# Layernorm applies ahead of the exponentials of k, k-v products in three groups, and another spread of the W_q folds

## The chip, the cores and the metric

The kernel runs on one core of one Trainium2 chip. The core has five engines with an instruction queue each: TensorE (PE in the profile; its weight loads stand as PEld), VectorE (DVE), ScalarE (ACT), GpSimd (POOL) and SyncE (SP, which here issues every DMA). Each queue runs in order; an instruction that waits for a semaphore holds back what stands behind it on its engine. The metric is device time in microseconds (us) of one execution, lower is better; the time of a kernel is the median of its runs.

## What is computed

Two blocks follow one another on x, 2048 rows of 640 features in bf16: a linear attention with 32 heads of 20 features, and a gated feed-forward of width 1536. Cut to what matters:

```python
qkv = (_layernorm(x) @ wqkv).reshape(B, S, 3, H, Dh)...
q, k, v = qkv[0], qkv[1], qkv[2]
pq = jnp.einsum("bhsd,hdf->bhsf", q, w_phi)
pk = jnp.einsum("bhsd,hdf->bhsf", k, w_phi)
phi_q = jnp.concatenate([_softmax(pq), _softmax(-pq)], axis=-1)
phi_k = jnp.concatenate([_softmax(pk), _softmax(-pk)], axis=-1)
kv = jnp.einsum("bhsf,bhsd->bhfd", phi_k, v)
z  = jnp.einsum("bhsf->bhf", phi_k)
num = jnp.einsum("bhqf,bhfd->bhqd", phi_q, kv)
den = jnp.einsum("bhqf,bhf->bhq", phi_q, z)[..., None] + 1e-6
h = x + (num / den)... @ wo
h2 = h + (_gelu(_layernorm(h) @ w_gate) * (_layernorm(h) @ w_up)) @ w_down
```

The change touches only the first half: the layernorm of x, k and v, the products of phi_k with v, and the preparation of the weights of q.

## The kernel before

The 2048 rows are 16 tiles of 128 rows (`NT`), in four blocks of four tiles. All engines run in the order in which the program names the instructions; nothing reorders them.

**Before the loop** the first tiles are loaded and normalised, their v is made, and W_k is folded with w_phi, so that k's features come out of one projection. That is what `fold` (L213) does for one chunk `d` of 128 rows of a weight: six small matmuls into a PSUM tile `wa` (L227), and a copy from there into the folded weight (L236 on ScalarE). W_q is folded in the loop: `FQ` gives the pass of each of its five chunks, `LQ` the pass in which SP issues the transposing load of the chunk (`load_T`, L186). All copies of W_q's folds are on ScalarE.

**The loop of 16 passes** (L440) is the place of the change. Pass t does, in this order:

1. `k_tile(t)` (L300): ten matmuls of the tile's normalised, transposed rows with the folded W_k into a PSUM tile `pk` (L272), then two exponentials on ScalarE, of pk and of -pk, into `E` (L305). They are called E(t) below.
2. A fold of W_q, if `FQ` has one for t; in pass 15 also the first four pieces of q's projection (`q_mm`, L360) and their exponentials (L365).
3. The k-v products of the tiles that `KVG` names for t (`kv_tile`, L332): 20 matmuls a tile, of E with `vt`, that add up over all 16 tiles in one PSUM tile `kvp` (L338). The tiles that are left follow behind the loop (L486).
4. `v_mm(t + 4)`: ten matmuls of the tile four ahead with W_v into a PSUM tile `pv` (L272). They need `LN1T` of that tile.
5. `ln_ap(t + 6)` (L256): ScalarE normalises the tile six ahead into `ln` (L133), with the bias `mr` that GpSimd has made (L127), and SP issues a DMA that writes its transpose into `LN1T` (L149).
6. `v_ev(t + 4)`: ScalarE copies pv into `vS` (L292).
7. In even passes `ln_st(t + 8, t + 9)` (L252): the statistics of two tiles, on VectorE (L109, L113) and GpSimd (L121, L122, and one `mr` for each tile, L127).
8. `k_norm(t)` (L308): VectorE sums E over the features (`sk`, L312) and takes the reciprocal (`rs`, L316); v is divided by it into `vt` (L320). One half of vt, for tiles of `VP` both, is GpSimd's; VectorE does its half one pass later, behind the sum of the next tile.

From pass 3 (`T3`) on the PSUM holds three tiles of the pool `psG`, which pk, wa, pv and pq take in turn, and `kvp`. A tile of the pool can be written again when the engine that reads it is through. E and vt have eight buffers each, so tile t takes the buffer of tile t - 8.

**Behind the loop** come the rest of the k-v products, `kv_mask` (L342: a small VectorE operation, a copy by ScalarE, and one masked product each on VectorE and GpSimd) into `KV`, the rest of q's projection, and the attention output and feed-forward, in which TensorE is the engine of almost every step.

The plan before the change, by pass:

```python
LQ = (7, 8, 9, 9, 10)
FQ = (10, 11, 12, 13, 14)
KVG = {5: (0, 1), 9: (2, 3, 4, 5), 13: (6, 7, 8, 9), 15: (10, 11)}
```

Of the kernel before, what the change touches and what calls it, by code (L numbers as in the profile page):

```python
# [17 lines left out]
def kernel(  # L18
# [19 lines left out]
    NT = S // P  # L38
# [7 lines left out]
    NH = [(P * c + P - 1) // Dh - H0[c] + 1 for c in range(NC)]  # L46
    VP = (0, 2, 4, 6, 9, 11)
    KA, QA = (0, 2, 4), (0, 1, 2, 3, 4)
    LQ = (7, 8, 9, 9, 10)
    FQ = (10, 11, 12, 13, 14)  # L50

    QG = ((0, 1), (2, 3), (4, 5), (6,), (7, 8), (9, 10), (11, 12), (13, 14), (15,), (16,), (17,), (18,), (19,))
    QT = (15, 15, 15, 15)
    T3 = 3

    KVG = {5: (0, 1), 9: (2, 3, 4, 5), 13: (6, 7, 8, 9), 15: (10, 11)}
    VC = Dh + 1
    KC = Dh + 2

# [39 lines left out]
    def gtile(name):  # L99
        return psG.tile([P, 2, 512], F32, name=name, tag="G")  # L100
# [40 lines left out]
    def transpose_to(dst, src, on_pe, on_dve=False):  # L141

        if on_pe:
            tp = psG.tile([P, 16, P], BF16, name="tp", tag="G")
            for c in range(NC):
                nc.tensor.transpose(tp[:, c, :], src[:, c * P:(c + 1) * P], ident)
            (nc.vector.tensor_copy if on_dve else nc.scalar.copy)(dst, tp[:, 0:NC, :])  # L147
        else:
            nc.sync.dma_start_transpose(dst, src)  # L149
# [63 lines left out]
    def fold(WT, W2, halves, ds=range(NC)):  # L213


        runs = []
        for c in range(NC):
            lo, hi = H0[c] * Dh, (H0[c] + NH[c]) * Dh
            for u in range(2):
                a, b = max(lo, u * HD), min(hi, (u + 1) * HD)  # L220
                if a < b:
                    runs.append((u, c, a, b))
        runs.sort()
        for d in ds:
            wa = gtile("wa")
            for i, (u, c, a, b) in enumerate(runs):
                nc.tensor.matmul(wa[:, u, a - u * HD:b - u * HD], lhsT=WT[:, c, d * P:(d + 1) * P],  # L227
                                 rhs=BD[:, c].rearrange("p a b -> p (a b)")[:, a - H0[c] * Dh:b - H0[c] * Dh],
                                 start=(i == 0 or runs[i - 1][0] != u),
                                 stop=(i + 1 == len(runs) or runs[i + 1][0] != u), skip_group_check=True)  # L230
            dst, src = W2[:, d, :].rearrange("p (u f) -> p u f", u=2), wa[:, :, 0:HD]
            if halves:
                dst = W2[:, d, :].rearrange("p (c u f) -> p u c f", c=NC, u=2)
                src = src.rearrange("p u (c f) -> p u c f", c=NC)
            if d in (QA if halves else KA):
                nc.scalar.copy(dst, src)  # L236
            else:
                nc.vector.tensor_copy(dst, src)
# [13 lines left out]
    def ln_st(*tiles, act=True, between=None, log=False):  # L252
        for t, v in zip(tiles, ln_stats(p1, [x_sb[t // 4][:, t % 4, :] for t in tiles], "1", act, between, log)):
            lnp[t] = v

    def ln_ap(t, on_act=False, on_pe=False):  # L256
        ln = (ln_act if on_act else ln_dve)(p1, "1", *lnp[t])
        if on_pe:
            lnp[t] = ln
        else:  # L260
            transpose_to(LN1T[t // 4][:, :, t % 4 * P:(t % 4 + 1) * P], ln, False)
# [8 lines left out]
    def proj(ps, t, W, us=(0, 1), rows=False):  # L270
        for u, c in sorted(((u, c) for u in us for c in range(NC)), key=lambda x: x[::-1] if rows else x):
            nc.tensor.matmul(ps[:, u, 0:HD], lhsT=lnT(t, c), rhs=W[:, c, u * HD:(u + 1) * HD],  # L272
                             start=(c == 0), stop=(c == NC - 1))
# [3 lines left out]
    def v_mm(t, us=(0, 1)):  # L277
        if 0 in us:
            pv[t] = gtile("pv")
        proj(pv[t], t, Wv, us)  # L280
# [10 lines left out]
    def v_ev(t):  # L291
        nc.scalar.activation(vS[t % 8][:, :, 0:Dh].rearrange("p (u h) f -> p u h f", u=2),  # L292
                             pv[t][:, :, 0:HD].rearrange("p u (h f) -> p u h f", f=Dh), ACTF.Copy,
                             scale=lnp[t][2] if t in CT else 1.0)
# [5 lines left out]
    def k_tile(t):  # L300
        pk = gtile("pk")
        proj(pk, t, Wk2, rows=t == 0)
        Ek[t] = ev.tile([P, 2, D], BF16, name="E", bufs=8)
        for s in range(2):
            nc.scalar.activation(Ek[t][:, s, :].rearrange("p (u f) -> p u f", u=2), pk[:, :, 0:HD],  # L305
                                 ACTF.Exp, scale=((lnp[t][2], nrstd[t]) if t in CT else (1.0, -1.0))[s])

    def k_norm(t):  # L308


        sk = small(p1, [P, 2 * H], "sk")
        nc.vector.reduce_sum(sk, Ek[t].rearrange("p s (h f) -> p (s h) f", f=Dh), axis=AX.X)  # L312
        if t - 1 in todo:
            todo.pop(t - 1)()
        rs = small(p1, [P, 2 * H], "rs")
        nc.vector.reciprocal(rs, sk)  # L316
        Vt[t] = vt = ev.tile([P, 2, H, VC], BF16, name="vt", bufs=8)

        def mult(s, eng):
            eng.tensor_tensor(vt[:, s], vS[t % 8], rs[:, s * H:(s + 1) * H, None].to_broadcast([P, H, VC]), ALU.mult)  # L320

        mult(1, nc.gpsimd)
        if t in VP:
            mult(0, nc.gpsimd)
        elif t == NT - 1:
            mult(0, nc.vector)
        else:
            todo[t] = lambda: mult(0, nc.vector)
# [3 lines left out]
    def kv_tile(t):  # L332

        for s in range(2):
            for c in range(NC):
                for u in range(2):
                    f0, h0 = u * HD + c * 64, u * UH + 3 * c
                    nc.tensor.matmul(kvp[HALF[u], s, c * 4 * VC:(c + 1) * 4 * VC],  # L338
                                     lhsT=Ek[t][:, s, f0:f0 + 64], rhs=Vt[t][:, s, h0:h0 + 4, :],
                                     start=(c == 0 and t == 0), stop=(t == NT - 1), skip_group_check=True)  # L340
# [13 lines left out]
    def q_mm(j):  # L354

        pqs[j] = gtile("pq")
        for i, bc in enumerate(QG[j]):
            b, c = divmod(bc, NC)
            for kc in range(NC):
                nc.tensor.matmul(pqs[j][:, i, :], lhsT=Wq2[:, kc, c * P:(c + 1) * P], rhs=LN1T[b][:, kc, :],  # L360
                                 start=(kc == 0), stop=(kc == NC - 1))

    def q_exp(j, signs=(0, 1)):
        for s in signs:
            nc.scalar.activation(Eq[j][:, :, s, :], pqs[j][:, 0:len(QG[j])], ACTF.Exp, scale=(1.0, -1.0)[s])  # L365
# [74 lines left out]
    for t in range(NT):  # L440
        if t == T3:
            ps_cm.close()
            psG = ps_cm.enter_context(tc.tile_pool(name="psG", bufs=3, space=PSUM, reuse_waits="tile"))
            psK = ps_cm.enter_context(tc.tile_pool(name="psK", bufs=1, space=PSUM, reuse_waits="tile"))
            kvp = psK.tile([P, 2, 512], F32, name="kvp")
        k_tile(t)
        if t == 0:
            ln_ap(6)
        if t in FQ:
            fold(WqT, Wq2, True, [i for i, f in enumerate(FQ) if f == t])  # L450
        for j in range(len(QT)):
            if t == QT[j]:
                q_mm(j)
                q_exp(j)
        for i in KVG.get(t, ()):
            kv_tile(i)
        if 0 < t < NT - 4:
            v_mm(t + 4)
        if t > 0 and t + 6 < NT:
            ln_ap(t + 6, on_act=True)  # L460
        if 0 < t < NT - 4:
            v_ev(t + 4)
        if t % 2 == 0 and t + 8 < NT:
            ln_st(t + 8, t + 9)
        k_norm(t)
        load_T(WqT, 0, *[i for i, f in enumerate(LQ) if f == t])
        if t == 10:

            for i in CT:
                ln_ap(i)  # L470
        if t == 9:
            nc.gpsimd.memset(KV, 0.0)
            nc.gpsimd.memset(kmask, 1.0)
            for r in HALF:
                nc.gpsimd.affine_select(out=kmask[r], in_=kmask[r], pattern=[[4, NC], [-Dh, 4]],
                                        compare_op=ALU.is_ge, fill=0.0, base=0, channel_multiplier=1)
                nc.gpsimd.affine_select(out=kmask[r], in_=kmask[r], pattern=[[-4, NC], [Dh, 4]],
                                        compare_op=ALU.is_ge, fill=0.0, base=Dh - 1, channel_multiplier=-1)
            nc.gpsimd.tensor_copy(KV[:, :, 0, :, KC - 1], kmask)
            nc.gpsimd.tensor_copy(KV[:, :, 1, :, 0], kmask)  # L480
        if t == 13:
            nc.sync.dma_start(Wg, wg_v)
            nc.sync.dma_start(Wo, wo_v)
            nc.sync.dma_start(Wu, wu_v)
    q = len(QT)
    for t in range(12, NT):  # L486
        kv_tile(t)
    kv_mask()
    ev_cm.__exit__(None, None, None)
# [323 lines left out]
```

## Time and profile before

| | |
|---|---|
| median of 3 runs | 278.11 us (277.75 to 278.13) |
| the profiled execution, its time | 277.38 us |
| its span, first to last instruction | 275.7 us |
| granted TensorE clock | 1.00 |
| first loop, from pk(0) to the last k-v product | 16.5 to 70.05 us |
| ScalarE, two exponentials of a pass (L305) | 1.30 us |
| ScalarE, one ln (L133) | 0.92 us |
| ScalarE, one copy of pv (L292) | 0.71 us |
| VectorE, sum of a tile's E (L312) | 1.43 us |
| GpSimd, half of a tile's vt (L320) | 1.31 us |
| LN1T from issue to landing, median and longest | 2.6 and 4.3 us |

The profile is one execution of the program, taken by the hardware. Lines of the timeline are: start, length, engine, line, operation, output and inputs, shapes, how many in a row, and in brackets how long the engine had been idle and what released it. Lines of the chain of waits are: start, length, what. Matmuls are pipelined: ten projection matmuls take 1.36 us from the start of one group to the start of the next, though each is shown with its full length of 0.30. ScalarE's instructions overlap at their ends too, so its steps are read from start to start. A part of the execution's time lies outside the span, 1.68 us here.

### The profile page before, as it was taken

The page shows a single profiled execution, that of the slowest core. Times are in us where ns is not written, and L with a number is a line of the kernel's source. Part 1 is how long each engine was busy: PE and PEld are TensorE (multiplying, and loading weights), DVE is VectorE, ACT ScalarE, POOL GpSimd, SP SyncE. Part 2 cuts the span into 40 slices and gives each one's busy share as a digit, 9 for nine tenths or more (in the row PEclk, how much of TensorE's full clock was granted, in tenths as well). Part 3 has the DMA queues.
Part 4 walks back from the last instruction along what each step waited for, and adds up shares of the span by engine and source line. Part 5 has one row for each costly group of instructions (what it writes and reads, how often), then busy time and mean ns, then how long its engine had stood idle before and what let it go on. Part 6 is the DMA issues. An engine that isn't in the chain of part 4 may idle for free.

```text
span 275.7 us, 5930 instructions
## 1 busy us (share of the span) xinstructions
PE 269.6 (98%) x2335; PEld 173.7 (63%) x2348; DVE 177.5 (64%) x336; ACT 138.3 (50%) x238; POOL 96.4 (35%) x218
## 2 busy tenths in 40 slices
PE   7999999999999999999999999999999999999995
PEld 4777667775555887788764555675555576444574
DVE  6899999999496876675468763356866332333322
ACT  4879897879598755374552345223154500232100
POOL 4248897765202227365312552101175300000000
PEclk9999999999999999999999999999999999999999
DMA  7962626589820022324111142110223111000011
GB/s 199 200 244 55 74 52 112 80 259 395 277 76 0 4 50 42 79 49 76 33 41 48 26 73 48 49 50 2 55 45 69 24 48 50 25 0 0 0 50 48
DMA packets 42235, 21.37 MB, mean 78 GB/s; under 512 B 35040, under 2 KB 40416, under 8 KB 42208
## 3 DMA queue, kind: packets, MB, share of 16 engines
q1 hardware_dynamic: 42208, 21.01, 30.3%
q8 instruction: 18, 0.29, 0.5%
q14 instruction: 9, 0.07, 0.1%
HBM read 10.18 MB, written 2.62 MB: 46 GB/s over the span
## 4 chain that ended last, share of the span: by engine, by line
PE 88%; ACT 4%; DVE 3%; DMA 2%; issue 1%; POOL 0%
PE gu L658 38%; PE pd L677 19%; PE pq L360 8%; PE po L601 8%; PE pk L272 5%; PE pv L272 5%; PE ab L529 3%; PE kvp L338 2%; ACT E L305 2%; DMA LN1T<-ln 2%; ACT ln L133 1%; DMA x_sb<-in_A_x_dram 1%; PE wa L227 1%; DVE statsc L109 1%; DVE stats L109 1%
## 5 line engine op out<-in xcount | busy, mean ns | idle before, releaser
L661 ACT ACTIVATE g<-gu 128x512 bf16<-128x512 f32 (+1 forms) x60 | 30.8, 513 | 69.1 <-PE gu L658 68.2
L664 DVE TENSOR_TENSOR GT<-gu,g 128x512 bf16<-128x512 f32 (+1 forms) x60 | 34.4, 580 | 48.2 <-PE gu L658 39.3
L658 PE MATMUL gu<-LN2T,Wg 128*128 128x512 bf16 (+1 forms) x291 | 61.3, 335 | 0.6
L658 PE MATMUL gu<-LN2T,Wu 128*128 128x512 bf16 (+1 forms) x300 | 61.7, 336 | 0.0
L677 PE MATMUL pd<-Wd,GT 128*128 128x320 bf16 (+2 forms) x396 | 53.5, 295 | 0.0
L677 PEld LDWEIGHTS <-GT 128*128 128x128 bf16 x396 | 37.9, 98 | 14.7 <-DVE GT L664 0.2
L658 PEld LDWEIGHTS <-Wu 128*128 128x128 bf16 x300 | 29.4, 98 | 22.6
L658 PEld LDWEIGHTS <-Wg 128*128 128x128 bf16 x300 | 28.9, 98 | 21.4
L272 PEld LDWEIGHTS <-LN1T 128*128 128x128 bf16 x290 | 27.8, 98 | 11.0 <-DMA LN1T<-ln 0.7
L680 DVE TENSOR_TENSOR y<-pd,x_sb 128x320 bf16<-128x320 f32 (+2 forms) x29 | 13.9, 480 | 29.0 <-PE pd L677 29.0
L320 POOL TENSOR_TENSOR vt<-vS,rs 128x672 bf16<-128x672 bf16 x22 | 29.1, 1344 | 9.1 <-DVE rs L316 7.4
L601 PE MATMUL po<-Wo,oT 128*128 128x320 bf16 x160 | 24.3, 299 | 0.0
L272 PE MATMUL pk<-Wk,LN1T 128*128 128x320 bf16 x160 | 24.2, 299 | 0.0
L360 PE MATMUL pq<-LN1T,Wq 128*128 128x512 bf16 x96 | 22.7, 379 | 0.2
L312 DVE TENSOR_REDUCE sk<-E 128x64 f32<-128x1280 bf16 x16 | 22.9, 1430 | 0.0
L365 ACT ACTIVATE Eq<-pq 128x1024 bf16<-128x1024 f32 (+1 forms) x26 | 19.9, 829 | 2.3 <-PE pq L360 2.3
L601 PEld LDWEIGHTS <-oT 128*128 128x128 bf16 x160 | 15.6, 98 | 7.4 <-ACT oT L147 0.3
L305 ACT ACTIVATE E<-pk 128x640 bf16<-128x640 f32 x28 | 18.4, 716 | 3.9 <-PE pk L272 3.8
L272 PE MATMUL pv<-Wv,LN1T 128*128 128x320 bf16 x130 | 19.8, 299 | 0.3 <-DMA LN1T<-ln 0.3
L578 DVE TENSOR_TENSOR tt<-AB,w 128x1280 bf16<-128x1280 f32 x12 | 17.9, 1488 | 1.1 <-POOL w L571 0.9
L133 ACT ACTIVATE ln<-x_sb,v,rstd 128x640 bf16<-128x640 bf16 x14 | 12.9, 920 | 10.7 <-POOL v L637 10.3
L360 PEld LDWEIGHTS <-Wq 128*128 128x128 bf16 x100 | 9.5, 98 | 10.4 <-issue 0.2
(110 smaller groups left out, 292.2 us busy)
## 6 DMA issues: line engine op xcount, KB each, us to landing
out_dram<-y SPq DMA_DIRECT2D x15, 160.0 KB, 1.8
Wg<-in_B_w_gate_dram SPq DMA_DIRECT2D x1, 1920.0 KB, 8.6
Wu<-in_B_w_up_dram SPq DMA_DIRECT2D x1, 1920.0 KB, 14.6
Wd<-in_B_w_down_dram SPq DMA_DIRECT2D x1, 1920.0 KB, 7.9
x_sb<-in_A_x_dram SPq DMA_DIRECT2D x2, 640.0 KB, 6.0
Wo<-in_A_wo_dram SPq DMA_DIRECT2D x1, 800.0 KB, 10.3
x_sb<-in_A_x_dram SPq DMA_DIRECT2D x4, 160.0 KB, 3.1
Wv<-in_A_wqkv_dram SPq DMA_DIRECT2D x2, 320.0 KB, 4.2
```

The lines of the kernel that those rows point to most:

```text
L272: nc.tensor.matmul(ps[:, u, 0:HD], lhsT=lnT(t, c), rhs=W[:, c, u * HD:(u + 1) * HD], start=(c == 0), stop=(c == NC - 1))
L305: nc.scalar.activation(Ek[t][:, s, :].rearrange("p (u f) -> p u f", u=2), pk[:, :, 0:HD], ACTF.Exp, scale=((lnp[t][2], nrstd[t]) if t in C ...
L312: nc.vector.reduce_sum(sk, Ek[t].rearrange("p s (h f) -> p (s h) f", f=Dh), axis=AX.X)
L320: eng.tensor_tensor(vt[:, s], vS[t % 8], rs[:, s * H:(s + 1) * H, None].to_broadcast([P, H, VC]), ALU.mult)
L360: nc.tensor.matmul(pqs[j][:, i, :], lhsT=Wq2[:, kc, c * P:(c + 1) * P], rhs=LN1T[b][:, kc, :], start=(kc == 0), stop=(kc == NC - 1))
L365: nc.scalar.activation(Eq[j][:, :, s, :], pqs[j][:, 0:len(QG[j])], ACTF.Exp, scale=(1.0, -1.0)[s])
L578: nc.vector.tensor_tensor(tt.rearrange("p s (h f) -> p s h f", f=Dh), num, w[:, :, :, None].to_broadcast([P, 2, H, Dh]), ALU.mult)
L601: nc.tensor.matmul(pos[u], lhsT=st[t][:, c, :], rhs=Wo[:, c, u * HD:(u + 1) * HD], start=(c == 0), stop=(c == NC - 1))
L658: nc.tensor.matmul(gu[i][:, 0:n], lhsT=W[:, c, f * P:(f + 1) * P], rhs=LN2T[b][:, c, a0:a1], start=(c == 0), stop=(c == NC - 1))
L661: nc.scalar.activation(g[:, 0:n], gu[0][:, 0:n], ACTF.Gelu_apprx_tanh)
L664: nc.vector.tensor_tensor(st[b, "g", f][:, a0:a1], gu[1][:, 0:n], g[:, 0:n], ALU.mult)
L677: nc.tensor.matmul(ps, lhsT=st[b, "g", f][:, tl * P:(tl + 1) * P], rhs=Wd[:, f, f0:f1], start=(f == 0), stop=(f == NF - 1))
```

## The change

Four tables or orders change; no instruction is added or removed.

- `ln_ap(t + 6)` moves, in passes 2 to 9, from behind v's matmuls to the head of the pass, ahead of `k_tile(t)`. On ScalarE the ln then stands ahead of E(t); on SP the transpose of LN1T is issued from there. Pass 1 keeps the old place.
- The k-v products run in passes 7 (tiles 0 to 3) and 11 (4 to 7) and, for tiles 8 to 15, behind the loop. Before, they ran in passes 5, 9, 13 and 15 and behind the loop; those of 15 and those behind the loop follow one another.
- The folds of W_q are in passes 8, 10, 11, 12, 14 instead of 10 to 14.
- The transposing loads of W_q are in passes 5, 7, 8, 9, 10 instead of 7, 8, 9, 9, 10.

```diff
-    LQ = (7, 8, 9, 9, 10)
-    FQ = (10, 11, 12, 13, 14)
+    LQ = (5, 7, 8, 9, 10)
+    FQ = (8, 10, 11, 12, 14)
...
-    KVG = {5: (0, 1), 9: (2, 3, 4, 5), 13: (6, 7, 8, 9), 15: (10, 11)}
+    KVG = {7: (0, 1, 2, 3), 11: (4, 5, 6, 7)}
...
+        if t >= 2 and t + 6 < NT:
+            ln_ap(t + 6, on_act=True)
         k_tile(t)
...
-        if t > 0 and t + 6 < NT:
+        if 0 < t < 2 and t + 6 < NT:
             ln_ap(t + 6, on_act=True)
...
-    for t in range(12, NT):
+    for t in range(8, NT):
         kv_tile(t)
```

## The prediction

> **What bounds the kernel.** I read the page's busy table and its chain first. TensorE is busy for nearly the whole span, and the chain that ended last is TensorE for 88% of it.
>
> ```profile
> PE 269.6 (98%) x2335; PEld 173.7 (63%) x2348; DVE 177.5 (64%) x336; ACT 138.3 (50%) x238; POOL 96.4 (35%) x218
> PE 88%; ACT 4%; DVE 3%; DMA 2%; issue 1%; POOL 0%
> ```
>
> So the change can gain only where TensorE pauses, and loses wherever it makes TensorE pause. The change touches passes 2 to 15 of the first loop, from 20.6 us to 70 us, so I then read that stretch engine by engine. The chain of waits in order of time shows what TensorE lost there (start, length, what):
>
> ```profile
> 27.09 4.32 DMA LN1T<-ln
> 31.46 1.53 PE pv L272 x10
> ...
> 39.78 1.53 PE pv L272 x10
> 41.31 1.36 PE pk L272 x10
> 42.67 1.65 PE kvp L338 x80
> ...
> 67.53 2.52 PE kvp L338 x120
> ```
>
> An undisturbed group of ten projection matmuls takes 1.36 us from start to start (36.90 to 38.26 in the timeline). pv(9), at 31.46, started 0.43 us late: the 40 k-v matmuls before it began at 30.20 and need some 0.82. It waited for LN1T, whose layernorm ended at 27.07. pv(12) started 0.16 late (38.26 + 1.36 = 39.62 against 39.78), also on LN1T. These 0.59 us are all that is lost on TensorE in the loop, up to its last products.
>
> At the end of the loop there is a second bound. VectorE is busy 3.9 to 4.0 us of every 4 us from 20 to 68, and its order is fixed; the last product of the loop waits for it and GpSimd. GpSimd's vt for tile 15 is this line:
>
> ```profile
> 67.65 1.97 POOL L320 TENSOR_TENSOR vt<-vS,rs 128x672 bf16<-128x672 bf16 x1 [1.35 <-PE pq L360]
> ```
>
> It ends at 69.62. The k-v matmuls then follow one another within 30 ns, except one pair, 69.56 and 69.67: kv(15) already waits 0.10 us for this vt. What TensorE gains earlier is lost here, unless VectorE's row moves too.
>
> **What the change costs, part by part.** The decisive place is pass 8, in the timelines of TensorE, ScalarE, GpSimd and VectorE:
>
> ```profile
> 38.26 1.52 PE L272 MATMUL pk<-Wk,LN1T 128*128 128x320 bf16 x10
> 41.15 1.52 PE L272 MATMUL pk<-Wk,LN1T 128*128 128x320 bf16 x10
> ```
>
> ```profile
> 39.82 1.30 ACT L305 ACTIVATE E<-pk 128x640 bf16<-128x640 f32 x2
> 41.32 0.92 ACT L133 ACTIVATE ln<-x_sb,mr,rstd 128x640 bf16<-128x640 bf16 x1 [0.20 <-POOL mr L127]
> 42.15 0.69 ACT L292 ACTIVATE vS<-pv 128x640 bf16<-128x640 f32 x1
> ```
>
> ```profile
> 39.59 0.71 POOL L122 TENSOR_TENSOR rstd<-ve,nhalf 128x2 f32<-128x2 f32 x1
> 40.40 0.89 POOL L127 TENSOR_SCALAR mr<-mv,rstd 128x1 f32<-128x1 f32 x1
> ```
>
> ```profile
> 40.30 0.85 DVE L320 TENSOR_TENSOR vt<-vS,rs 128x672 bf16<-128x672 bf16 x1
> ```
>
> The reader is to see that ln(14) needs mr(14), which GpSimd ends at 41.29, and that ScalarE today does E(8) first, at 39.82, and even then waits 0.20 us. Statistics are made in pairs in even passes, so the same holds in passes 4 and 6: mr(10) ends at 28.59, while E(4) starts at 27.60; mr(12) ends at 34.94, E(6) starts at 34.39. VectorE and GpSimd make them; their rows keep their order and are full, so I keep these times.
>
> *Layernorm ahead of the exponentials.* ScalarE's work stays the same; its steps start-to-start are ln 0.81, first E 0.60, second E 0.585 (0.70 long), v copy 0.59, fold copy 0.57. Queued behind the waiting ln are E(t), the fold copy and v's copy, and behind these TensorE, which has three PSUM buffers ("pk", "wa", "pv" in turn) and reuses one 0.05 us after ScalarE let it go (5.92 to 5.97 for the first transpose). In passes 2 and 3 mr is there; E comes 0.81 later, pv(7) still finds its buffer (24.55 against 24.68). Pass 4: ln(10) at 28.62, E(4) at 29.43 and 30.03, over at 30.73. pv(9) takes pk(4)'s buffer: TensorE is there at 28.75 + 1.36 = 30.11 and goes on at 30.78, a **new wait of 0.67**. From there: pk(6) 32.14, pv(10) 33.50, pk(7) 34.86, then the first k-v group 36.31 to 37.96 (it covers E(6), over at 37.08, which pv(11) needs), pk(8) 39.33.
>
> *The fold in pass 8* puts one more buffer between pk(8) and pk(9): wa at 40.69, pv(12) at 41.00, and pk(9), due at 42.36, gets pk(8)'s buffer, where without the fold it would get pv(11)'s. ScalarE: ln(14) at 41.32, E(8) at 42.14 and 42.73, over at 43.43. pk(9) starts at 43.48: a **new wait of 1.12**. This instant is set by mr(14) whatever TensorE lost before; without the wait at pv(9) this one is 1.79.
>
> *Earlier LN1T.* ln(9) starts at 24.89 instead of 26.06, ln(12) at 34.97 instead of 35.57; even with the slowest landing of the trace, 4.32, they are there before 30.3 and 40.2, ahead of pv(9) and pv(12). Both old waits go: **-0.59**.
>
> *k-v groups.* All 320 matmuls stay. A group of 80 takes 1.65 (42.60 to 44.25), one of 120 takes 2.52 less the 0.10 of waiting; so 40 are 0.77, a group costs 0.10 by itself, and 0.09 passes before its first matmul (41.15 + 1.36 = 42.51, start 42.60). One group fewer: **-0.19**. All vt that the groups need are done some us before (vt(3) at 34.8, vt(7) at 46.3), and E and vt buffers are freed before passes 8 and 12 ask for them. After the loop 8 tiles run instead of 6, so that kv(15) comes after vt(15): **-0.10**, the old wait.
>
> *Folds and loads.* Five folds of 0.31 us and five copies stay. Each W_q transpose issue holds SP for 1.27 us beside 1.20 for each LN1T, 2.5 in a pass of 2.7 or more, as in passes 7 and 8 today; LN1T has over 1 us to spare, so I cost the reordering at nothing; without that cover it is at most the 1.2 us of one issue ahead of pv(12), which then still ends inside pk(9)'s wait for mr(14). Behind pass 9 I followed TensorE and ScalarE through passes 10 to 15 in the same way: pk(11), pk(14) and pq(0) find their buffers 0.12 us before they need them, pk(15) 0.02. Bounds: nothing, and 0.4 if all four are late by 0.1 more.
>
> **Sum.** 0.67 + 1.12 - 0.59 - 0.19 - 0.10 = +0.91. By the clock of the run: from pk(9) to the projection after the last product, 41.15 to 69.98, is 28.83; the new one has 40 products, a group's overhead, a fold and the wait less, 0.77 + 0.19 + 0.31 + 0.10 = 1.37; 43.48 + 27.46 = 70.94, 0.96 later. What follows is TensorE without slack: q's projection at 69.98, products with KV at 72.25, which is ready at 71.81; all of it moves along. The profiled execution took 277.38 with a span of 275.70; I expect a span of about 276.6 and 278.3 for it. The median of the runs, 278.11, is 0.73 above that execution; with +0.93 it becomes 279.0.
>
> **The unknown price** is mr(14). Its line shows 0.89; the shortest of its kind is 0.26, and it ran beside VectorE's vt. With 0.26 it ends at 40.66, pk(9) starts at 42.85, and the sum is +0.33. I take 0.89, since both starts come from rows that the change leaves as they are.
>
> The Trainium skill ("SBUF — State Buffer", Who interferes with whom) says that a VectorE instruction with two SBUF inputs and a GpSimd instruction that reads SBUF hold a port in turn, and the one that starts second blocks until the first is over. The 0.89 agrees, ending 0.14 after vt. By that rule mr would take its 0.26 if it came 0.1 us earlier, and the sum would be the +0.33 above. A second rule speaks against any new pause: "TensorE: Matmul & The Clock Gate" (Why this matters for your kernels) warns of gaps over about 3 us, after which the clock halves. The granted clock is 1.00 through the 0.43 us wait here; 1.12 is longer than this but below the rule's figure, which adds nothing to the sum.
>
> **Rivals.**
> 1. *ScalarE's waits on even passes* (forecast): 279.0, from 278.6 to 279.7. Chance 0.67.
> 2. *mr is early enough*, or ScalarE catches up more than I count: +0.3, 278.4. For it: the overlap on GpSimd is a matter of 0.1 us. Against: its rows are locked to VectorE's. Chance 0.11.
> 3. *No stall at all*: the statistics are ready when ln asks for them, the LN1T waits vanish. Not slower: -0.78 on TensorE, but the last vt allows -0.1 only: 278.0; if VectorE's row also shortens, 277.4. It decides if mr(14) ends before 40.1, when ScalarE is done with v(11). Against it: ln(14) waits today, 1.2 us later in the row. Chance 0.10.
> 4. *The stalls spread*: E is so late that passes 10 to 15 miss their margins of 0.02 to 0.12 us, and VectorE's reduce(9) (margin 0.06) slips too: +0.4 more, 279.5 to 279.9. Chance 0.12.
>
> A difference of 0.2%, 0.56 us, is about what can be told from none. Faster (under 277.55): 0.06, most of case 3. Same: 0.16, from 3, 2 and the edge of 1. Slower: 0.78. The range 278.2 to 279.9 leaves out case 3 and a little above case 4, together under 2 in 10.
>
> **What would show it.** In the profile after: ScalarE idle ahead of ln (L133) in passes 4, 6 and 8, put down to GpSimd's mr, about 1.2 us in each of passes 4 and 8; TensorE paused about 1.1 us ahead of pk(9), released by E; no wait of pv on LN1T; kvp in groups of 80, 80 and 160, the last without a pause. Wrong if GpSimd's mr(14) ends well before 41.3, if pk(9) starts before 42.5, or if VectorE's row ends more than 0.3 us from 68.4.

## The result: 0.84 us slower

The changed kernel took 278.58 us (median of 12 runs, 278.13 to 279.2), the kernel before, beside it on the same chip, 277.74 us (12 runs, 277.45 to 278.14). The ratio is 1.0029, with a 95% interval of 1.0021 to 1.0037: 0.58 to 1.03 us slower. The forecast was 0.91 to 0.96 us slower; its 279.0 us was counted from the 278.11 us of the first three of these 12 runs of before, which is why the measured 278.58 lies further below it than the difference does.

The profiled execution of after took 278.13 us with a span of 276.4. The page's busy table and its chain (share of the span by engine):

```profile
PE 270.5 (98%) x2348; PEld 174.4 (63%) x2348; DVE 177.6 (64%) x336; ACT 137.8 (50%) x238; POOL 96.5 (35%) x218
PE 85%; DVE 9%; POOL 2%; issue 2%; ACT 1%; DVEq 0%
```

TensorE's busy share says nothing: it is 98% in both. The chain does. Before, it ran over TensorE from 31 us on, but for 0.5 us; now VectorE and GpSimd hold part of it, up to 43 us. In order of time (start, length, what) it shows where it crosses over to TensorE:

```profile
39.42 0.72 POOL rstd L122
...
40.23 0.89 POOL mr L127
...
41.15 0.92 ACT ln L133
42.07 0.36 ACT E L305
...
42.55 0.70 ACT E L305
43.26 0.04 issue
43.30 1.52 PE pk L272 x10
```

The timelines of ScalarE and of TensorE in pass 8 have the same place with its idle times in brackets:

```profile
41.15 0.92 ACT L133 ACTIVATE ln<-x_sb,mr,rstd 128x640 bf16<-128x640 bf16 x1 [1.06 <-POOL mr L127]
41.97 1.27 ACT L305 ACTIVATE E<-pk 128x640 bf16<-128x640 f32 x2
```

```profile
40.83 1.52 PE L272 MATMUL pv<-Wv,LN1T 128*128 128x320 bf16 x10
43.30 1.52 PE L272 MATMUL pk<-Wk,LN1T 128*128 128x320 bf16 x10 [0.95 <-ACT E L305]
```

Before, ScalarE did E(8) at 39.82 and only then waited 0.20 us for mr(14). Now ln(14) stands ahead and waits 1.06, E(8) starts at 41.97, and pk(9), due at 40.83 + 1.36 = 42.18, starts at 43.30: 1.12 us late. (The bracket counts from the modelled end of the matmul before, so it is shorter.) The granted clock is 1.00 from 42 to 44 us, through this pause. The other new wait is ahead of pv(9), in pass 5:

```profile
28.82 1.52 PE L272 MATMUL pk<-Wk,LN1T 128*128 128x320 bf16 x10
30.61 0.57 PE L272 MATMUL pv<-Wv,LN1T 128*128 128x320 bf16 x3 [0.26 <-ACT E L305]
```

Due at 30.18, it starts at 30.61, 0.43 late. In this profile no matmul of the loop waits for LN1T any more, and the products behind the loop run as one group without a pause:

```profile
67.55 3.24 PE L338 MATMUL kvp<-vt,E 128*64 128x84 bf16 x160
70.72 2.33 PE L360 MATMUL pq<-LN1T,Wq 128*128 128x512 bf16 x10
```

**A yardstick.** Executions differ by up to 1.3 us in when the loop's work on VectorE begins: the first sum of E (sk(0), L312) starts between 20.30 and 21.61 in the profiles of this study, and this shifts all that hangs on VectorE. The four latest (ln_only, rstd_twice, after_act01 and odd_only, 4.7 to 5.1 us after pk(0) and not 3.8 to 4.1) are those in which VectorE's statistics before the loop wait 0.8 to 1.2 us for a load of x; in before that wait is 0.16 us. So spans of single profiles can't be compared to 0.1 us. Two distances can: from the start of sk(0) to the start of q's projection behind the loop, read from the timelines, and from there to the end of the span, which is 205.69 us in both kernels (202.83 of it up to the last y, the last instruction that computes). For after, sk(0) is this line, and the projection the one at 70.72 above:

```profile
20.45 1.43 DVE L312 TENSOR_REDUCE sk<-E 128x64 f32<-128x1280 bf16 x1
```

The distance is 50.27; before it was 69.98 - 20.62 = 49.36. The loop is 0.91 us longer by this measure, 0.68 us longer when counted from pk(0) (54.13 against 53.45).

| kernel | sk(0) | end of the last vt | q's projection | sk(0) to projection | median against before, us |
|---|---|---|---|---|---|
| before | 20.62 | 69.62 | 69.98 | 49.36 | |
| after | 20.45 | 69.46 | 70.72 | 50.27 | +0.84 |
| ln_only | 21.53 | 70.54 | 70.90 | 49.37 | +0.14 |
| no_ln | 20.93 | 69.95 | 71.12 | 50.19 | +0.31 |
| fold9 | 20.85 | 69.88 | 70.99 | 50.14 | +0.74 |
| kv5 | 20.30 | 69.28 | 70.56 | 50.27 | +0.85 |
| rstd_twice | 21.37 | 71.15 | 72.42 | 51.05 | +2.17 |
| before_act01 | 20.74 | 67.94 | 70.61 | 49.87 | +0.92 |
| stats_early | 20.79 | 71.52 | 71.89 | 51.10 | +2.04 |
| stats_early_act01 | 20.62 | 69.51 | 70.25 | 49.62 | +0.12 |
| after_act01 | 21.55 | 70.09 | 71.83 | 50.27 | +0.75 |
| odd_only | 21.61 | 70.62 | 70.99 | 49.38 | +0.17 |
| odd_act01 | 20.49 | 68.44 | 69.11 | 48.62 | -1.16 |

### The profile page after: what moved, and what is told of

Its sections match the earlier page's. It is cut to its first block, busy times and chain, and to the rows that moved or that the text cites. A ratio compares the mean times of both kernels' runs of the same rounds, so it can differ in the third digit from the quotient of the medians.

```text
span 276.4 us, 5940 instructions
## 1 busy us (share of the span) xinstructions
PE 270.5 (98%) x2348; PEld 174.4 (63%) x2348; DVE 177.6 (64%) x336; ACT 137.8 (50%) x238; POOL 96.5 (35%) x218
## 2 busy tenths in 40 slices
DMA packets 42235, 21.37 MB, mean 77 GB/s; under 512 B 35040, under 2 KB 40416, under 8 KB 42208
## 4 chain that ended last, share of the span: by engine, by line
PE 85%; DVE 9%; POOL 2%; issue 2%; ACT 1%; DVEq 0%
PE gu L660 38%; PE pd L679 19%; PE pq L360 8%; PE po L603 8%; PE pk L272 3%; DVE stats L109 3%; PE ab L531 3%; DVE sk L312 2%; PE kvp L338 2%; PE pv L272 2%; PE wu L209 1%; POOL vt L320 1%; DVE rs L316 1%; PE tp L146 1%; POOL rstd L122 1%
## 5 line engine op out<-in xcount | busy, mean ns | idle before, releaser
L312 DVE TENSOR_REDUCE sk<-E 128x64 f32<-128x1280 bf16 x16 | 23.0, 1435 | 0.0
```

## The experiments

### The parts of the change

**ln_only**: the kernel before with the move of ln alone.

```diff
+        if t >= 2 and t + 6 < NT:
+            ln_ap(t + 6, on_act=True)
         k_tile(t)
...
-        if t > 0 and t + 6 < NT:
+        if 0 < t < 2 and t + 6 < NT:
```

> The kernel before with one part of the change: ln ahead of E in passes 2 to 9. Theory (ScalarE's waits for mr cost only where the PSUM buffer of the late E is asked for soon; the old k-v groups in passes 5 and 9 and the absence of a fold in pass 8 put work between): ScalarE waits 1 us each in passes 4, 6 and 8, TensorE's waits on LN1T vanish, a wait of about 0.4 us for E(6) comes ahead of pv(11), nothing before pk(9); with the last vt as a floor the time is that of before, -0.1 to +0.1 us. Rival (the order on ScalarE alone is what costs): +0.7 to +1.0 us.

Measured: 277.77 us beside 277.63 (ratio 1.0005, 0.9994 to 1.0016). Its waits from 26 to 46 us (what for, us in total, times, longest):

```profile
ACT ln L133 <- POOL mr L127: 3.2, 3, 1.1
...
PE pv L272 <- ACT E L305: 0.7, 1, 0.7
```

ScalarE waits for mr three times, up to 1.1 us, much as in after (0.73, 1.06 and 1.06), and the kernel is not measurably slower. A wait of ScalarE is not a wait of TensorE: here the products in passes 5 and 9 fill the time. pv(11) is 0.90 us late (expected 0.4), and this too is lost in the distance to the last vt, 49.37 as before. The profiled execution is the slowest of the 12, 278.31 us, with a late sk(0) (5.00 us after pk(0), 4.09 in before), so that TensorE has some 0.9 us more to lose there; for the usual execution only the median speaks.

**no_ln**: the kernel after with ln at its old place.

```diff
-        if t >= 2 and t + 6 < NT:
-            ln_ap(t + 6, on_act=True)
         k_tile(t)
...
-        if 0 < t < 2 and t + 6 < NT:
+        if t > 0 and t + 6 < NT:
```

> The kernel after with ln put back behind v's matmuls; groups, folds and loads stay as changed. Theory: no wait for mr ahead of E, so none of 1.1 us ahead of pk(9); without the products in pass 5, pv(9) asks for LN1T 0.8 us earlier than before and waits 0 to 1.3 us for it, by the landing: 0 to +0.5 us against before. Rival (the later k-v products and the eight tiles behind the loop are what costs): +0.8 us or more, as after.

Measured: 277.94 beside 277.63 (1.0013, 1.0004 to 1.0022). The wait ahead of pk(9) is gone; the one for LN1T came, in the profile just above the 0 to 1.3 us that were expected:

```profile
29.30 1.52 PE L272 MATMUL pk<-Wk,LN1T 128*128 128x320 bf16 x10
32.04 1.12 PE L272 MATMUL pv<-Wv,LN1T 128*128 128x320 bf16 x7 [1.22 <-DMA LN1T<-ln]
```

pv(9) is due at 29.30 + 1.36 = 30.66 and starts 1.38 late. This too is the slowest of 12 executions, 278.53 us, and its loop is 0.83 us longer than before's; the median is only 0.31 above, so this wait is probably shorter in most executions, which no trace shows. By the medians, then, neither the move of ln nor the rest of the change costs 0.8 us alone. The wait at pk(9) takes both: the late E, and its buffer asked for before products fill the time.

**fold9**: the kernel after, the first fold one pass later.

```diff
-    FQ = (8, 10, 11, 12, 14)
+    FQ = (9, 10, 11, 12, 14)
```

> The kernel after with the first fold of W_q in pass 9 instead of 8. Prediction's reading (the fold's buffer makes pk(9) wait for E(8)): pk(9) no longer waits, 1.1 us come back, the time is that of before, 0 to -0.1. Rival (ScalarE's backlog after ln(14) is the limit, and the wait only moves to pv(13) and pk(10)): small waits at wa, pv(13) and pk(10) add up to nearly the same, pk(10) starts only 0.1 us earlier than after; +0.6 to +0.8 us against before.

Measured: 278.37 beside 277.63 (1.0028, 1.0018 to 1.0038). The rival held. TensorE's timeline from pk(9) on:

```profile
42.27 1.52 PE L272 MATMUL pk<-Wk,LN1T 128*128 128x320 bf16 x10
43.70 0.47 PE L227 MATMUL wa<-BD,WqT 128*128 128x140 bf16 x6
44.30 1.52 PE L272 MATMUL pv<-Wv,LN1T 128*128 128x320 bf16 x10
46.28 0.98 PE L272 MATMUL pk<-Wk,LN1T 128*128 128x320 bf16 x6 [0.47 <-ACT E L305]
```

pk(9) waits no more, but wa is 0.07 late (42.27 + 1.36 against 43.70), pv(13) 0.29 (43.70 + 0.31), and pk(10) 0.62 (44.30 + 1.36): 0.98 in all, for 1.12 before. What is late after ln(14) is ScalarE's whole queue, E(8), v(12), ln(15), E(9); the fold's buffer only decided which of these TensorE meets first. From sk(0) to the projection 0.13 us come back.

**kv5**: the kernel after, tiles 0 and 1 back in pass 5.

```diff
-    KVG = {7: (0, 1, 2, 3), 11: (4, 5, 6, 7)}
+    KVG = {5: (0, 1), 7: (2, 3), 11: (4, 5, 6, 7)}
```

> The kernel after with the products of tiles 0 and 1 back in pass 5, tiles 2 and 3 in pass 7. Theory (the start of pk(9) is set by mr(14), whatever TensorE lost before): the wait ahead of pv(9), 0.43 us, goes, and the time stays that of after, within 0.2 us, with a longer wait ahead of pk(9) or the same work done in it. Rival (the two waits add): 0.4 us faster than after, less a group's 0.2.

Measured: 278.48 beside 277.63 (1.0035, 1.0023 to 1.0047). The wait ahead of pv(9) is gone, and pk(9) waits 1.30 us instead of 1.12 (40.49 + 1.36 against 43.15):

```profile
40.49 1.52 PE L272 MATMUL pv<-Wv,LN1T 128*128 128x320 bf16 x10
43.15 1.52 PE L272 MATMUL pk<-Wk,LN1T 128*128 128x320 bf16 x10 [1.13 <-ACT E L305]
```

pk(9) starts 22.85 us after sk(0), as in after, and sk(0) to projection is 50.27 as in after. The two waits don't add: the time is set by pk(9). That pk(9) is set by mr(14) is what the next two kernels test.

### The price of mr(14), and its lateness

**rstd_twice**: the kernel after, the power instruction ahead of mr(14) made twice.

```diff
-            nc.gpsimd.tensor_tensor(rstd, ve, nhalf[:, 0:n], op=ALU.pow)
+            for _ in range(2 if twice else 1):
+                nc.gpsimd.tensor_tensor(rstd, ve, nhalf[:, 0:n], op=ALU.pow)
...
-        for t, v in zip(tiles, ln_stats(..., log)):
+        for t, v in zip(tiles, ln_stats(..., log, 14 in tiles)):
```

> The kernel after with the 0.71 us power instruction of GpSimd made twice for tiles 14 and 15, ahead of mr(14). If mr(14)'s 0.89 us are 0.26 of its own and the rest a block by VectorE's vt beside it, it now starts as that vt ends and takes about 0.3: it ends 0.2 us later, and the time is 0.2 us above after (+1.0 against before). Rival (0.89 is its own): it ends 0.8 later, 0.8 above after (+1.6 against before). Either way the time follows the end of mr(14) one for one; if it doesn't move at all, pk(9) is not set by mr(14).

Measured: 279.51 beside 277.34 (1.0072, 1.0058 to 1.0086), so some 1.3 above after. GpSimd, and VectorE beside it:

```profile
40.35 2.10 POOL L123 TENSOR_TENSOR rstd<-ve,nhalf 128x2 f32<-128x2 f32 x2
42.55 0.50 POOL L128 TENSOR_SCALAR mr<-mv,rstd 128x1 f32<-128x1 f32 x2
```

```profile
41.05 0.85 DVE L321 TENSOR_TENSOR vt<-vS,rs 128x672 bf16<-128x672 bf16 x1
```

Two instructions that take 0.71 each take 2.10 together, and two mr take 0.50, where in after the first alone took 0.89. VectorE's vt now runs beside the second power instruction, and the 0.6 us of block moved there. So 0.89 is 0.27 and a block of 0.62, as the first theory says; but my 0.2 us for the end of mr(14) was wrong, since the inserted instruction took the block itself. mr(14) ends 1.77 us after VectorE's vt starts, against 0.98 in after, 0.79 more, and the loop is 0.78 longer (51.05 against 50.27): one for one. Of the 1.3 us between the medians this leaves some 0.5, which this profile doesn't explain.

**stats_early**: the kernel after, statistics of tiles 10 to 15 one pass earlier.

```diff
-        if t % 2 == 0 and t + 8 < NT:
-            ln_st(t + 8, t + 9)
+        if t in (0, 1, 3, 5):
+            i = t + 9 if t else 8
+            ln_st(i, i + 1)
```

> The kernel after with the statistics of tiles 10 to 15 made one pass earlier (passes 1, 3 and 5 instead of 2, 4 and 6), so that mr is there when ln asks for it. Theory: no wait for mr, none of 1.1 us ahead of pk(9); from the first sum of E to the projection behind the loop it takes 49.4 us as before, not 50.3, since the last vt is the floor; 0.0 (-0.2 to +0.2) against before, -0.8 against after. Rival (mr is not the cause of after's loss): +0.8 against before.

Measured: 279.38 beside 277.34 (1.0064, 1.0051 to 1.0077), far off what was expected. VectorE's row, from the first sum to the last, took 45.85 us instead of 44.13. Three of its vt grew:

```profile
27.78 1.47 DVE L320 TENSOR_TENSOR vt<-vS,rs 128x672 bf16<-128x672 bf16 x1
...
34.75 1.46 DVE L320 TENSOR_TENSOR vt<-vS,rs 128x672 bf16<-128x672 bf16 x1
...
41.70 1.32 DVE L320 TENSOR_TENSOR vt<-vS,rs 128x672 bf16<-128x672 bf16 x1
```

They take 0.85 each in before and after, where they run beside GpSimd's mr and block it; here GpSimd's vt is under way when they come, and they are the ones held up: 0.62 + 0.61 + 0.47 = 1.70 us, the growth of the row. The last vt then ends at 71.52, and the loop with it. mr's slowness was the other side of VectorE's speed.

Nor did mr(14) come a pass earlier. It ends 20.01 us after sk(0), against 20.66 in after: its statistics are ready at 38.44, but on GpSimd two vt stand ahead of it until 39.34. So pk(9) still comes 0.88 us late (40.75 + 1.36 against 42.99):

```profile
40.53 0.50 POOL L127 TENSOR_SCALAR mr<-mv,rstd 128x1 f32<-128x1 f32 x2
```

```profile
40.75 1.52 PE L272 MATMUL pv<-Wv,LN1T 128*128 128x320 bf16 x10
42.99 1.52 PE L272 MATMUL pk<-Wk,LN1T 128*128 128x320 bf16 x10 [0.72 <-ACT E L305]
```

pk(9) starts 22.20 us after sk(0), against 22.85 in after: mr(14) and pk(9) are both 0.65 us earlier, one for one again, now in the other direction.

### The floor at the end of the loop

Four kernels move the layernorms of tiles 0 and 1 (1.1 us each on VectorE, pass 10) to ScalarE, which needs an mr for each:

```diff
-        if t == 10:
-
-            for i in CT:
-                ln_ap(i)
...
+        if t == 11:
+            for i in CT:
+                ln_ap(i, on_act=True)
         if 0 < t < NT - 4:
             v_mm(t + 4)
...
+        if t == 8:
+            for i in CT:
+                nc.gpsimd.tensor_scalar(lnp[i][3], lnp[i][1], lnp[i][2], -1.0, op0=ALU.mult, op1=ALU.mult)
         k_norm(t)
```

**before_act01**: this on the kernel before.

> The kernel before with the layernorms of tiles 0 and 1 (two instructions of 1.09 us on VectorE in pass 10) moved to ScalarE in pass 11, and their two mr made on GpSimd in pass 8. Theory (before, VectorE's row from its first sum of E to the last vt sets the end of the loop, TensorE only 0.1 us behind it): vt(15) ends some 2 us earlier, TensorE takes over as the bound, -0.1 to -0.4 us against before. Rival (TensorE alone bounds the loop): 0.

Measured: 278.26 beside 277.34 (1.0030, 1.0020 to 1.0039). The last vt ends earlier as expected, 47.20 us after sk(0) instead of 49.00, but TensorE pays in pass 12:

```profile
52.76 0.48 PE L227 MATMUL wa<-BD,WqT 128*128 128x140 bf16 x6
54.09 1.52 PE L272 MATMUL pk<-Wk,LN1T 128*128 128x320 bf16 x10 [0.84 <-ACT vS L292]
```

Before has no products in pass 11 that would cover two more layernorms on ScalarE; pk(13) comes 1.0 us late. A gain that puts its cost in a place without slack, where both the theory and its rival had expected no loss. The loop is 0.51 us longer by sk(0) to projection. Another 0.37 us of the 0.92 lies outside the span: 2.09 us in the median of its executions, 1.72 in before's. No run shows why.

**stats_early_act01**: on stats_early.

> Both edits on the kernel after: statistics one pass earlier, and the layernorms of tiles 0 and 1 on ScalarE. Theory: neither mr nor the last vt binds, TensorE's savings show for the first time (0.59 us of waits on LN1T, 0.19 of a k-v group, 0.10 of the last vt): -0.7 to -1.1 us against before. Rival (these savings are no real ones): 0, as before_act01 at best.

Measured: 277.46 beside 277.34 (1.0001, 0.9992 to 1.0010): 1.9 us below stats_early, which is what VectorE's row lost (44.01 against 45.85), but no gain over before. Expected was -0.7 to -1.1. pk(9) still waits 0.88 us for E(8), because ln(14) ahead of it still waits for mr(14), 0.51 us, which ends 20.01 us after sk(0) as in stats_early. The last vt no longer holds the end, and sk(0) to projection shows the rest: 49.62, which is 0.65 less than in after, as much as mr(14) and pk(9) are earlier.

**after_act01**: on the kernel after, whose products in pass 11 do cover it.

> The kernel after with the layernorms of tiles 0 and 1 moved from VectorE (pass 10) to ScalarE (pass 11, where the k-v products give ScalarE 1.6 us of idle time), so that the last vt ends 1.8 us earlier. Theory (after is set by mr(14) and pk(9), TensorE behind it is without slack to the end): no change against after, +0.7 to +0.9 us against before. Rival (after is held by VectorE's row at the end too): 0.5 us or more below after.

Measured: 278.46 beside 277.71 (1.0023, 1.0011 to 1.0035), sk(0) to projection 50.27, exactly that of after, though the last vt ends 0.47 us earlier against sk(0) (1.8 was expected). After is not held by the last vt; pk(9) starts 22.85 us after sk(0) here too.

**odd_only**: the kernel after with ln ahead of E in odd passes alone, where mr is long made.

```diff
-        if t >= 2 and t + 6 < NT:
+        if t >= 2 and t % 2 and t + 6 < NT:
             ln_ap(t + 6, on_act=True)
...
-        if 0 < t < 2 and t + 6 < NT:
+        if (t == 1 or t > 1 and t % 2 == 0) and t + 6 < NT:
```

> The kernel after with ln ahead of E in the odd passes 3 to 9 alone, where mr has been made two passes before; in even passes ln stands behind v's matmuls as before. Theory: no wait for mr ahead of E, no wait on LN1T ahead of pv(9), no pause ahead of pk(9); TensorE comes to the last product some 0.6 us earlier than before and waits there for the last vt: 49.4 us from the first sum of E to the projection behind the loop, as before; 0 against before (-0.2 to +0.2). Rival (TensorE's own row sets the end): -0.5 to -0.8.

Measured: 277.88 beside 277.71 (1.0005, 0.9995 to 1.0015).

```profile
66.81 3.07 PE L338 MATMUL kvp<-vt,E 128*64 128x84 bf16 x150
70.67 0.38 PE L338 MATMUL kvp<-vt,E 128*64 128x84 bf16 x10 [0.79 <-POOL vt L320]
```

The last ten products wait 0.79 us for GpSimd's vt(15). TensorE's gain is there and is lost at the floor: 49.38. (In this execution, one with a late sk(0), LN1T also made TensorE wait twice, 0.58 us ahead of pv(6) and 0.29 ahead of pv(12).)

**odd_act01**: odd_only with the two layernorms on ScalarE.

> odd_only with the layernorms of tiles 0 and 1 on ScalarE in pass 11. Theory: the floor of the last vt is 1.8 us lower, and TensorE's savings show: -0.5 to -0.9 us against before, and faster than both kernels. Rival (another wait takes their place, as ScalarE's did in before_act01): 0.

Measured: 276.55 beside 277.71 (0.9959, 0.9946 to 0.9972), 1.16 us faster than before, and so faster than both kernels, and by more than the 0.5 to 0.9 us expected. In its profile no matmul of the loop is listed as waiting, the products run through, and the chain of the page is TensorE for 94%:

```profile
65.94 3.24 PE L338 MATMUL kvp<-vt,E 128*64 128x84 bf16 x160
69.11 2.12 PE L360 MATMUL pq<-LN1T,Wq 128*128 128x512 bf16 x8
```

```profile
PE 94%; DVE 3%; DMA 1%; issue 1%; POOL 0%; ACT 0%
```

The distance is 48.62, 0.74 less than before. Another 0.29 us is gained between the projection and the end of the span (205.40 instead of 205.69), in all four kernels with this edit. It lies behind the last y, which ends 202.83 us after the projection as in before; what makes that end shorter no run shows. The rest of the 1.16 may be executions with a late sk(0), which no longer set the end; this is argued, not shown.

## Why the prediction held, step by step

- *The wait at pk(9)*, +1.12: measured 1.12. Against sk(0) it was forecast at 43.48 - 20.62 = 22.86 and came at 22.85. That mr(14) sets it whatever TensorE lost before: kv5 removes the earlier wait and changes nothing; rstd_twice moves mr(14) by 0.79 and the loop by 0.78; the two stats_early kernels move mr(14) and pk(9) by -0.65, and the loop too where the last vt doesn't hold it. (The 0.05 us for a buffer was read at a matmul that waited for ScalarE's data and not for a buffer; in after's chain it is 0.04.)
- *The wait at pv(9)*, +0.67: measured 0.43. In this execution VectorE's row stood 0.24 us earlier against TensorE's than in the one of before (sk(0) 3.86 us behind pk(0), not 4.09; in before VectorE had waited 0.16 us for a load of x). This differs between executions, and the forecast could not know it. As kv5 shows, its size doesn't matter.
- *LN1T*, -0.59: the waits are gone. *One group fewer and the old wait for the last vt*, -0.19 and -0.10: the last group has no pause, and the whole loop from sk(0) is 0.91 longer, which is the sum. Counted from pk(0) it is 0.68 longer, and that is the sum with 0.43 in place of 0.67.
- *The price of mr(14)*, taken as 0.89 and not 0.26: measured 0.89 in after. The block by VectorE's vt, which the Trainium skill ("SBUF — State Buffer", Who interferes with whom) describes as a port held by the one that starts first, is seen from both sides: GpSimd blocked 0.62 in after, VectorE blocked 0.47 to 0.62 in stats_early.
- *The step that failed* is the one on the fold: "The fold in pass 8 puts one more buffer between pk(8) and pk(9)". That is how TensorE meets the late E(8), but not why it loses the time. fold9 takes this buffer away and gets back 0.10 of 0.84 us, since ScalarE's queue is behind as a whole; 0.98 us of waits stay, at wa, pv(13) and pk(10).
- *The case of no stall*: it was said that without stalls the last vt would allow -0.1 only, and more if VectorE's row shortens. odd_only is 0.17 above before, within its interval, and odd_act01 1.16 below.
- *Passes 10 to 15*, four margins of 0.02 to 0.12 us: no wait showed there in after.
- *The signs*: ScalarE's wait for mr was forecast at about 1.2 us in each of passes 4 and 8; it was 0.73 in pass 4, 1.06 in pass 8, and 1.06 in pass 6, where the products of pass 7 cover it. The other loads of W_q were not tested by themselves; no fold of after waits for them.

## What to carry to other kernels

Before an instruction is put ahead of others on an engine that runs in order, look up when its latest input is made and what stands behind it: here the ln itself was early work, but its bias was made by two engines whose rows run some 3 us behind (before, E(6) is over at 35.68 and its sum starts at 38.95), and everything queued behind it took on their lateness. A wait on a side engine costs nothing until the bound engine asks for what it holds, so the same wait cost nothing that the medians show with matmuls between (ln_only) and 0.8 us without. And when a gain on the busiest engine doesn't show, look at the last thing that it waits for at the end of the stage: only with that floor lowered too did the gain appear.

## What was not expected of the hardware

- In before, ln_only and odd_only the time from VectorE's first sum to the end of the loop is 49.36 to 49.38 us, although TensorE is busy for 98%, and the chain of before is TensorE's for 88%. Two engines of 64% and 35% busy share set the end of the loop; the last products wait 0.10 us for them in before and 0.79 in odd_only.
- The port block moves rather than goes: 0.62 us on GpSimd's mr in after, 0.60 on a power instruction when one is put in its place, 0.47 to 0.62 on VectorE's own vt when GpSimd starts first.
- The start of sk(0) varies from 20.30 to 21.61 us between executions whose first k projection starts between 16.46 and 17.08; in the latest ones VectorE waited for a load of x.
